# The first turn of an inverse transform in tiles of 32 rows by 64 columns, and some idle products in small tile shapes

## The chip, the cores and the metric

The kernel runs on one NeuronCore of one Trainium2 chip. It is one launch, with the inputs and the output in device memory, everything in float32. The metric is the device time of one execution in microseconds (us). Three executions of the kernel before took 675.04, 676.41 and 678.37 us; the median, 676.41 us, is its time.

The engines are called PE (TensorE, products into PSUM), DVE (VectorE), ACT (ScalarE), POOL (GpSimd) and SP (SyncE, here only a queue of transfers).

## The reference

Two residual blocks over 2048 tokens of 640 channels, with modulation rows computed from a vector `c`. Cut to what matters:

```python
x = A_q                                                     # (1, 2048, 640)
mod = (silu(c) @ w_mod).reshape(1, 6, 1, -1)                # sa, ca, ga, sb, cb, gb
h = layernorm(x) * (1 + ca) + sa
x = x + ga * A(h, A_k, A_v, A_shift_k, A_ssm_k, A_ssm_D)    # first block
h = layernorm(x) * (1 + cb) + sb
x = x + gb * B(h, B_w1, B_b1, B_w2, B_b2)                   # second block

def A(q, k, v, shift_k, ssm_k, ssm_D):
    kv = short_causal_conv(k, shift_k) * v                  # 4 taps in each channel
    y = irfft(rfft(kv, 4096) * rfft(ssm_k, 4096))[:2048]    # long causal convolution per channel
    return q * (y + kv * ssm_D)

def B(x, w1, b1, w2, b2):                                   # mixes tokens, channel by channel
    h = layernorm(x)
    u = gelu(einsum("bsd,sf->bdf", h, w1) + b1)             # 1728 hidden units
    return (einsum("bdf,fs->bds", u, w2) + b2).transpose(0, 2, 1)
```

## The kernel before

The first 280 us are block A, the rest block B. Block A works on channels in five chunks of 128, numbered 0 to 4 (`for c in range(NC)`, NC = 5). The long convolution of a chunk is a transform in two turns, a pointwise product and an inverse in two turns, all of them as f32 products on PE:

- `step1(side, t)` (line 223): the first turn forward, of the kernel (`side` 1) or of `kv` (`side` 0); 16 products a call with weights of 128 rows by 64 columns and 128 moving columns, four calls (`t`) for each side. ACT copies the result to `Z` (line 229).
- `f2(g)` (line 242): the second turn forward, 32 products a call with weights of 128 rows by 64 columns and 64 moving columns, in the two column halves of the array in turn; eight calls a chunk. ACT copies one half of each result (line 246), DVE multiplies both spectra (`mul`, line 57), POOL adds into `Y` (`add`).
- `i2(r)` (line 271): the first turn of the inverse, two calls a chunk, 64 products each. The 128 rows of `Y` are four independent strips of 32 rows (`qd`); a product takes 32 rows of `Y`, two of its columns blocks `i` at a time, as 128 weight columns, and 64 columns of the constant `V2` as the moving side. Each strip has its own PSUM bank. Four copies on ACT (line 280; in the last chunk's second call two of them on DVE, line 278) bring the result to `T2`.
- `i1(half)` (line 291): the second turn of the inverse, two calls a chunk, 64 products each with weights of 64 rows by 64 columns, in the four quarters of the array in turn. DVE multiplies the result by the modulated `q` straight from PSUM (`gate`).

All the order is written by hand; each engine works through its own list. In chunks 1 to 3 the list of PE is: eight `f2`, `step1(0,0)`, `step1(0,1)`, `i2(0)`, `step1(0,2)`, `i2(1)`, `step1(0,3)`, `i1(0)`, `step1(1,0)`, `i1(1)`, `step1(1,1)` to `step1(1,3)`, where `step1` already works for the next chunk. ACT's list there has the copies of `step1(0,0)` and `(0,1)`, the reordering of the next chunk's kernel (`perm`, line 168, two instructions), the four copies of `i2(0)`, the copy of `step1(0,2)`, the four of `i2(1)`. In chunk 0 the products for the modulation rows (`mod_part`, line 351) follow `step1(0,3)` on PE, and `mod_row` (362) after them gives the rows `G0`, `G1` that the gated product needs. In chunk 4 `mod_part` stands between the two calls of `i2`.

PSUM is eight banks: a ring of three slots of two banks, taken in turn by each call of `psum()`, and one slot for the taps. `i2` takes two slots, the others one.

At the very start PE has ten products of 128 x 128 by 512 columns whose result nobody reads (line 497, called idle products below), while the inputs are loaded; the first real work on PE is `step1(1,0)`.

The lines that the change touches, with the functions around them:

Of the kernel before, what the change touches and what calls it, by code (L numbers as in the profile page):

```python
# [47 lines left out]
def mixer_kernel(ctx: ExitStack, tc: tile.TileContext, q, k, v, shift_k, ssm_k, ssm_D, w1, b1, w2, b2, c,  # L48
# [7 lines left out]
    act, dve, pool, pe, sync = nc.scalar, nc.vector, nc.gpsimd, nc.tensor, nc.sync  # L56
# [3 lines left out]
    def mem(tag, n, name=None):  # L60

        return sb.tile([128, n], F32, name=name or tag, tag=tag, bufs=1)
# [4 lines left out]
    def psum(slot=None):  # L67

        uid[0] += 1
        slot = ring[uid[0] % len(ring)] if slot is None else slot  # L70
        return psp.tile([128, 1024], F32, name=f"pst_{uid[0]}", tag=f"pst{slot}", bufs=1)
# [5 lines left out]
    T_in, P, X, T_aux, T_kt = mem("in", 4288), mem("p", 2048), mem("x", 2048), mem("aux", 4096), mem("kt", 1536)  # L77
# [18 lines left out]
    Y = T_y.rearrange("p (r i k) -> p r i k", r=2, i=32)  # L96
# [3 lines left out]
    F1, V2, ID, OWN = SM[:, 0:256], SM[:, 256:384], SM[:, 384:420], SM[:, 420:422]  # L100
# [46 lines left out]
    def load_taps(c, eng=sync):  # L147
        for h in range(2):
            eng.dma_start(TR[64 * h:64 * h + 64], dram(shift_k, (DC * c + 64 * h) * 4, [[0, 64], [1, 256]]))
# [26 lines left out]
    def kv_ops(g, eng=dve, x=X, kx_=KX):  # L176
        S_, T_, W_ = (SV, TV, TAP) if eng is dve else (PS_.rearrange("p (n i) -> p n i", i=64),
                                                       PT.rearrange("p (n i) -> p n i", i=64), PW)
        pairs = lambda t: t.rearrange("p n (i e) -> p n i e", e=2)
        w = lambda s: W_[:, None, s, :].to_broadcast([128, 8, 64])  # L180
        kx = lambda s: kx_[:, 8 * g + 3 - s:8 * g + 11 - s, :]
        ops = [lambda: TT(eng, S_, kx(3), w(3), ALU.mult)]
        for s in (2, 1, 0):
            ops.append(lambda s=s: TT(eng, T_, kx(s), w(s), ALU.mult))
            ops.append(lambda: TT(eng, S_, S_, T_, ALU.add))
        ops.append(lambda: TT(eng, x.rearrange("p (i n e) -> p n i e", i=32, e=2)[:, 8 * g:8 * g + 8],
                              pairs(S_), pairs(VX[:, 8 * g:8 * g + 8]), ALU.mult))
        return ops
# [74 lines left out]
    def i2(r, eng=None):  # L263

        pp = [psum(), psum()]
        for s in range(8):
            for ri in range(2):
                for qd in range(4):
                    p = slice(32 * qd, 32 * qd + 32)
                    o, i = 512 * (qd % 2) + 64 * s, 2 * (8 * r + s)  # L270
                    pe.matmul(pp[qd // 2][:, o:o + 64], Y[p, ri, i:i + 2].rearrange("p i k -> p (i k)"),  # L271
                              V2[p, 64 * ri:64 * ri + 64], start=ri == 0, stop=ri == 1)
        for qd in range(4):
            a = 16 * (qd // 2) + 8 * r
            o = T2[:, a:a + 8, :, qd % 2]
            i = pp[qd // 2][:, 512 * (qd % 2):512 * (qd % 2) + 512].rearrange("p (a m) -> p a m", a=8)
            if eng is not None and qd > 1:
                eng.tensor_scalar(o, i, 1.0, None, op0=ALU.mult)
            else:
                act.activation(o, i, AF.Copy)  # L280

    def i1(half, slot=None):

        ps = psum(slot)
        for jj in range(8):
            for ri in range(2):
                for e in range(2):
                    p = slice(64 * e, 64 * e + 64)
                    for b in range(2):
                        n2 = 16 * b + 8 * half + jj  # L290
                        pe.matmul(ps[64 * b:64 * b + 64, 512 * e + 64 * jj:512 * e + 64 * jj + 64],  # L291
                                  V1[p, ri, n2], T2[p, :, 32 * ri + n2], start=ri == 0, stop=ri == 1)
        return ps
# [198 lines left out]
    w2_load(0)  # L492
    all_taps()
    load_taps(1, pool)
    ps = psum()
    for _ in range(10):
        pe.matmul(ps[:, 0:512], T_in[:, 192:320], T_in[:, 192:704], start=True, stop=True)
    ops = kv_ops(1, pool, X0)
    run(ops[:5])
    perm_add(0)  # L500
# [48 lines left out]
    for c in range(NC):  # L549
# [44 lines left out]
        if c == 0:  # L594
# [3 lines left out]
            ps = psum()  # L598
            pe.transpose(ps[:, 0:36], stg, ID[0:36, 0:36])
            act.activation(cols, ps[:, 0:36], AF.Copy)  # L600
            act.activation(sil, cols[:, 30:35], AF.Silu)
            step1(0, 1)
            i2(0)
            step1(0, 2)
            i2(1)
            k0 = step1(0, 3, True)
            for kk in range(4):
# [50 lines left out]
        if c:  # L658
            dv(7 if cn is not None else 8)
            i2(0)  # L660
            if cn is None:
                mod_part(tap, 3, pl[3])
                i2(1, dve)
                t = mem("y", 4096, "wb2")
                blk[2] = j16(t[:, 0:2048]), j16(t[:, 2048:4096])
                split_rows(0, X, (2,))
                split_rows(1, T_aux[:, 0:2048], (2,))
                break
            run(po)
            step1(0, 2)  # L670
            i2(1)
            step1(0, 3)
            dv(3)
# [11 lines left out]
        for half in range(2):  # L685
            ps = i1(half)
# [37 lines left out]
    start = []  # L724
# [84 lines left out]
    ps = i1(1, s1)  # L809
# [151 lines left out]
    for f_ in range(4, NF - 1):  # L961
        if f_ == HALF:
            ps = psum().rearrange("p (h m) -> p h m", h=2)
# [5 lines left out]
        ps = psum().rearrange("p (h m) -> p h m", h=2)  # L969
# [131 lines left out]
    for s in range(NW):  # L1101
        i = NF + s
# [16 lines left out]
        for f_ in range(NF):  # L1119
            u = U[f_]  # L1120
            for k, (w, r) in enumerate(((wh, 0), (wh, 2), (wl, 0))):
                for h in range(2):
                    pe.matmul(acc[s][:, h, 0:320], w[:, f_].bitcast(F32R), u[r + h].bitcast(F32R),  # L1123
                              start=f_ == 0 and k == 0, stop=f_ == NF - 1 and k == 2)
# [39 lines left out]
def build(inputs):  # L1164
    import concourse.bacc as bacc

    nc = bacc.Bacc("TRN2", target_bir_lowering=False, num_devices=1)
    arrays, args = {}, []

    def add(name, a):  # L1170
        a = np.ascontiguousarray(a)
        arrays[f"in_{name}_dram"] = a
        args.append(nc.dram_tensor(f"in_{name}_dram", a.shape, mybir.dt.from_np(a.dtype), kind="ExternalInput").ap())

    for name in _INS:
        a = np.asarray(inputs[name])
        add(name, a.reshape(S, D) if name in ('A_q', 'A_k', 'A_v') else a)
    for name, a in _constants().items():
        add("const_" + name, a)
    args.append(nc.dram_tensor("out_0_dram", (S, D), F32, kind="ExternalOutput").ap())  # L1180
    with tile.TileContext(nc) as tc:
        mixer_kernel(tc, *args)
    return nc, arrays
# [8 lines left out]
```

## Time and profile before

| what | value |
|---|---|
| executions | 675.04, 676.41, 678.37 us |
| profiled execution, from first to last instruction | 673.9 us (its span is the only time that it has) |
| PE matmuls | 628.9 us busy, 9119 records |
| PE weight loads | 596.1 us busy, 9119 records |
| DVE, ACT, POOL | 497.5, 300.1, 133.5 us busy |
| line 242 (`f2`), matmul | 2560 records, 78.9 us busy, median length of one 222 ns |
| line 271 (`i2`), matmul | 1280 records, 40.2 us busy, median length of one 270 ns |
| line 291 (`i1`), matmul | 1280 records, 23.6 us busy, median length of one 216 ns |
| line 223 (`step1`), matmul | 1280 records, 78.3 us busy |
| line 497 (idle products), matmul | 20 records, 11.4 us busy, first at 6.06 us |
| packets of the instruction queue q8 | 71, 1.16 MB |
| mean granted PE clock | 0.979 of full |

One product of f32 in the code is two matmul records and two weight loads in the trace (line 271: 10 calls of 64 products, 1280 records). Matmuls overlap, so the length of one record is not the time that it costs; the distance from one start to the next is. The times of block A's chunks, by the starts of `f2`: chunk 0 at 35.1 us, 1 at 98.9, 2 at 147.95, 3 at 191.55, 4 at 237.66; block B's products begin at 281 us.

In the rows below, an idle time is given in brackets with what ended it; "issue" there means that the profile shows nothing that the engine waited for. Names are output<-input.

### The profile page before, as it was taken

To read this page: it belongs to the slowest core of one execution; us is meant where nothing else is said; L and a number is where in the kernel's file an instruction comes from. 1 tells how busy PE (TensorE), PEld (TensorE's weight loads), DVE (VectorE), ACT (ScalarE), POOL (GpSimd) and SP (SyncE) were. 2 spreads that over 40 slices of the span, in tenths; PEclk is the share of its full clock that TensorE was granted. 3 is DMA by queue.
4 is the path that set the end of the run, shared out by engine and by line. 5 is a ranking of instruction groups with operands and counts; after the bars stand their busy time and mean duration, and the time that the engine had idled before them with its cause. 6 is when DMAs were issued, how large, how long until landed. Compare 5 with 4: busy or idle time off the path is not lost.

```text
span 673.9 us, 20760 instructions
## 1 busy us (share of the span) xinstructions
PE 628.9 (93%) x9119; PEld 596.1 (88%) x9119; DVE 497.5 (74%) x869; ACT 300.1 (45%) x483; POOL 133.5 (20%) x157
## 2 busy tenths in 40 slices
PE   6878887999999998999899999999999999999997
PEld 2878576989989996799789889999999999999997
DVE  7798698889798379788866621231589969888895
ACT  1564474647557465447654222322344143333331
POOL 5772068126133241000000000000000430000000
PEclk9999899999999999698999999999999999999999
DMA  9999897475426252430308333334352626356601
GB/s 185 214 266 259 277 181 160 94 147 115 67 66 217 60 154 65 107 81 1 63 3 154 63 62 65 63 63 116 98 147 71 190 77 182 115 147 168 187 32 39
DMA packets 166538, 81.23 MB, mean 121 GB/s; under 512 B 90830, under 2 KB 156912, under 8 KB 166448
## 3 DMA queue, kind: packets, MB, share of 16 engines
q1 hardware_dynamic: 159276, 78.32, 47.8%
q10 hardware_dynamic: 6916, 1.31, 1.2%
q8 instruction: 71, 1.16, 0.7%
q0 software_dynamic: 256, 0.28, 0.2%
q14 instruction: 19, 0.16, 0.1%
HBM read 69.40 MB, written 10.49 MB: 119 GB/s over the span
## 4 chain that ended last, share of the span: by engine, by line
PE 67%; DVE 16%; ACT 6%; issue 4%; DMA 3%; SPq 2%; POOL 1%; ACTq 0%; DVEq 0%; POOLq 0%
PE pst L445 20%; PE pst L1046 16%; PE pst L1123 7%; PE pst L223 7%; PE pst L271 6%; PE pst L242 6%; DVE p L57 2%; PE pst L291 2%; ACT z L280 2%; DVE tap L57 2%; PE tap L351 2%; PE pst L919 1%; DVE kt L57 1%; DMA y<-in_A_ssm_k_dram 1%; DVE aux L57 1%
## 5 line engine op out<-in xcount | busy, mean ns | idle before, releaser
L242 PE MATMUL pst<-z,w 128*64 128x64 f32 x2560 | 78.9, 223 | 13.5 <-DVE p L57 7.6
L242 PEld LDWEIGHTS pst<-z,w 128*64 128x64 f32 x2560 | 76.7, 138 | 16.3 <-issue 8.8
L57 POOL TENSOR_TENSOR y<-p 128x256 f32<-128x256 f32 x72 | 51.2, 740 | 39.7 <-DVE p L57 39.4
L229 ACT ACTIVATE z<-pst 128x1024 f32<-128x1024 f32 (+2 forms) x45 | 43.0, 974 | 35.0 <-PE pst L223 34.9
L57 DVE TENSOR_TENSOR p<-pst,kt 128x512 f32<-128x512 f32 x80 | 50.7, 680 | 8.6 <-ACT kt L246 8.6
L882 ACT ACTIVATE pst<-pst,sm 128x640 f32<-128x640 f32 x13 | 10.0, 766 | 75.8 <-PE pst L445 75.8
L271 PEld LDWEIGHTS pst<-v,y 32*128 32x128 f32 x1280 | 38.2, 187 | 6.0 <-issue 5.6
L271 PE MATMUL pst<-v,y 32*128 32x64 f32 x1280 | 40.2, 272 | 3.0 <-issue 2.9
L1046 PE MATMUL pst<-r_z,m_w 128*128 128x320 f32 x222 | 41.6, 309 | 0.1
L246 ACT ACTIVATE kt<-pst 128x512 f32<-128x512 f32 x40 | 23.9, 597 | 33.9 <-PE pst L242 17.1
L223 PE MATMUL pst<-v,p 128*64 128x128 f32 x640 | 36.7, 274 | 1.6 <-ACT p L168 1.6
L223 PEld LDWEIGHTS pst<-v,p 128*64 128x64 f32 x640 | 34.8, 137 | 3.0 <-ACT p L168 2.6
L57 POOL TENSOR_TENSOR m_p<-u_i,r_z 128x320 f32<-128x320 f32 x1 | 0.9, 870 | 183.4 <-issue 183.4
L1034 ACT ACTIVATE m_w<-m_v 128x896 fp32r<-128x896 f32 x24 | 22.7, 951 | 31.5 <-PE pst L1046 16.8
L57 DVE TENSOR_TENSOR tap<-tap,kt 128x512 f32<-128x512 f32 x51 | 35.5, 697 | 1.3
L223 PE MATMUL pst<-v,x 128*64 128x128 f32 x512 | 34.2, 291 | 2.0 <-issue 1.5
L1046 PEld LDWEIGHTS pst<-r_z,m_w 128*128 128x128 f32 x222 | 34.8, 188 | 0.4 <-DVE m_w L57 0.4
L223 PEld LDWEIGHTS pst<-v,x 128*64 128x64 f32 x512 | 30.9, 147 | 3.2 <-issue 2.5
L280 ACT ACTIVATE z<-pst 128x512 f32<-128x512 f32 x38 | 20.9, 644 | 24.0 <-PE pst L271 24.0
L57 DVE TENSOR_TENSOR m_w<-m_v,m_w 128x896 fp32r<-128x896 f32 x24 | 27.9, 1165 | 2.5 <-ACT m_w L1034 2.1
L57 DVE TENSOR_TENSOR kt<-in,tap 128x512 f32<-128x512 f32 x42 | 28.8, 686 | 1.2
L445 PE MATMUL pst<-r_z,wb0b 128*128 128x320 f32 x180 | 28.2, 310 | 0.9 <-DVE u_x L57 0.9
(308 smaller groups left out, 1497.5 us busy)
## 6 DMA issues: line engine op xcount, KB each, us to landing
x<-in_B_w_dram SPq DMA_DIRECT2D x20, 512.0 KB
m_x<-xs SPq DMA_DIRECT2D x28, 160.0 KB
out_dram<-m_x SPq DMA_DIRECT2D x28, 160.0 KB
aux<-in_A_ssm_k_dram SPq DMA_DIRECT2D x8, 512.0 KB
m_v<-in_B_w_dram SPq DMA_DIRECT2D x9, 448.0 KB
in<-in_w_mod_dram SPq DMA_DIRECT2D x4, 960.0 KB
x<-in_B_w_dram SPq DMA_DIRECT2D x7, 448.0 KB
in<-in_A_v_dram SPq DMA_DIRECT2D x22, 128.0 KB
```

The lines of the kernel that those rows point to most:

```text
L57: TT = lambda eng, o, a, b, op: eng.tensor_tensor(o, a, b, op=op)
L223: pe.matmul(ps[64 * ri:64 * ri + 64, o:o + 255:2], lhs, F1[:, 128 * ri:128 * ri + 128], start=True, stop=True)
L229: act.activation(Z[:, side, t, :, k0:k1], ps.rearrange("p (a k e) -> p a k e", a=4, e=2)[:, :, k0:k1], AF.Copy)
L242: pe.matmul(ps[64 * h:64 * h + 64, o:o + 64], W2[k1 // 32][:, 2 * (k1 % 32) + ri], rhs, start=True, stop=True)
L246: act.activation(kt.rearrange("p (m i) -> p m i", i=32), pv[:, :, 1], AF.Copy)
L271: pe.matmul(pp[qd // 2][:, o:o + 64], Y[p, ri, i:i + 2].rearrange("p i k -> p (i k)"), V2[p, 64 * ri:64 * ri + 64], start=ri == 0, stop=ri ...
L280: act.activation(o, i, AF.Copy)
L291: pe.matmul(ps[64 * b:64 * b + 64, 512 * e + 64 * jj:512 * e + 64 * jj + 64], V1[p, ri, n2], T2[p, :, 32 * ri + n2], start=ri == 0, stop=r ...
L445: pe.matmul(ps[0:m, h, 0:320], w_.bitcast(F32R), r_[:, 320 * h:320 * h + 320].bitcast(F32R), start=first and i == 0, stop=last and i == 2)
L1034: act.activation(W[n][0].bitcast(F32R), A[p, w_], AF.Copy)
L1046: pe.matmul(bank[n], w[:, i].bitcast(F32R), r.bitcast(F32R), start=i == 0 and k == 0, stop=i == 6 and k == 2)
L1123: pe.matmul(acc[s][:, h, 0:320], w[:, f_].bitcast(F32R), u[r + h].bitcast(F32R), start=f_ == 0 and k == 0, stop=f_ == NF - 1 and k == 2)
```

## The change

`i2` gets a loop over `e`. Instead of two column blocks of `Y` as 128 weight columns, a product takes one as 64 weight columns, and writes PSUM partitions 0 to 63 (`e` = 0) or 64 to 127 (`e` = 1), that is through the left or the right column half of the array. The four row strips and the moving side stay as they are, and so do the PSUM banks, the copies behind and all their waits. A call has 128 products where it had 64.

Of the ten idle products five stay. The others are replaced by 64 products with 64 moving columns: 16 in tiles of 64 x 64, 32 in tiles of 64 rows by 32 columns, 16 in tiles of 64 x 64 that write every second PSUM column. For these a second PSUM slot is taken, which turns the ring of three on by one for everything behind.

```diff
@@ i2 @@
         for s in range(8):
             for ri in range(2):
-                for qd in range(4):
-                    p = slice(32 * qd, 32 * qd + 32)
-                    o, i = 512 * (qd % 2) + 64 * s, 2 * (8 * r + s)
-                    pe.matmul(pp[qd // 2][:, o:o + 64], Y[p, ri, i:i + 2].rearrange("p i k -> p (i k)"),
-                              V2[p, 64 * ri:64 * ri + 64], start=ri == 0, stop=ri == 1)
+                for e in range(2):
+                    for qd in range(4):
+                        p = slice(32 * qd, 32 * qd + 32)
+                        o, i = 512 * (qd % 2) + 64 * s, 2 * (8 * r + s) + e
+                        pe.matmul(pp[qd // 2][64 * e:64 * e + 64, o:o + 64], Y[p, ri, i],
+                                  V2[p, 64 * ri:64 * ri + 64], start=ri == 0, stop=ri == 1)
@@ before the first kv_ops @@
-    ps = psum()
-    for _ in range(10):
-        pe.matmul(ps[:, 0:512], T_in[:, 192:320], T_in[:, 192:704], start=True, stop=True)
+    ps, ps_ = psum(), psum()
+    kin = T_in[:, 192:704]
+    for _ in range(5):
+        pe.matmul(ps[:, 0:512], kin[:, 0:128], kin, start=True, stop=True)
+
+    lo = lambda a: slice(64 * a, 64 * a + 64)
+    for n in range(16):
+        a, b, o = n // 2 % 2, n % 2, 64 * (n // 4)
+        pe.matmul(ps[lo(b), 512 * a + o:512 * a + o + 64], kin[lo(a), o:o + 64], kin[lo(a), 256:320], start=True, stop=True)
+    for n in range(32):
+        a, b, o = n // 4 % 2, n % 4, 64 * (n // 8)
+        pe.matmul(ps[32 * b:32 * b + 32, 512 * a + o:512 * a + o + 64], kin[lo(a), o:o + 32], kin[lo(a), 256:320], start=True, stop=True)
+    for n in range(16):
+        a, b, o = n // 2 % 2, n % 2, 128 * (n // 4)
+        pe.matmul(ps_[lo(b), 512 * a + o:512 * a + o + 128:2], kin[lo(a), o // 2:o // 2 + 64], kin[lo(a), 256:320], start=True, stop=True)
```

Line 271 of the kernel before is line 272 after it, and the lines behind the idle products move on by 13.

On PE the list of chunk 2, from `step1(0,1)` to `i1(0)`, reads before (the shape is that of the output, `x2` means two calls in a row; of each call of `i2` the first two rows are shown, for strips 0 and 1 in one slot and 2 and 3 in the other, and 30 like them follow):

```order
L223 MATMUL pst_2486<-v,x 64x128 x16
L271 MATMUL pst_2513<-v,y 128x64 x2
L271 MATMUL pst_2514<-v,y 128x64 x2
...
L223 MATMUL pst_2585<-v,x 64x128 x16
L271 MATMUL pst_2603<-v,y 128x64 x2
L271 MATMUL pst_2604<-v,y 128x64 x2
...
L223 MATMUL pst_2673<-v,x 64x128 x16
L291 MATMUL pst_2698<-z,v 64x64 x64
```

and after the change (here 62 rows like the two shown follow in each call):

```order
L223 MATMUL pst_2802<-v,x 64x128 x16
L272 MATMUL pst_2829<-v,y 64x64 x2
L272 MATMUL pst_2830<-v,y 64x64 x2
...
L223 MATMUL pst_2965<-v,x 64x128 x16
L272 MATMUL pst_2983<-v,y 64x64 x2
L272 MATMUL pst_2984<-v,y 64x64 x2
...
L223 MATMUL pst_3117<-v,x 64x128 x16
L292 MATMUL pst_3142<-z,v 64x64 x64
```

The order of the calls is the same; a call of `i2` has 128 products for 64, each with an output of 64 partitions for 128.

At the start of PE's list, before:

```order
L497 MATMUL pst_125<-in 128x512 x10
L223 MATMUL pst_189<-v,p 64x128 x16
L223 MATMUL pst_207<-v,p 64x128 x16
L223 MATMUL pst_225<-v,p 64x128 x16
L223 MATMUL pst_243<-v,p 64x128 x16
```

and after:

```order
L499 MATMUL pst_125<-in 128x512 x5
L504 MATMUL pst_125<-in 64x64 x16
L507 MATMUL pst_125<-in 32x64 x32
L510 MATMUL pst_126<-in 64x64 x16
L223 MATMUL pst_249<-v,p 64x128 x16
```

Five products of 512 columns have gone, 64 of 64 columns have come; what follows is the same.

## The prediction, made before the changed kernel was run

> **What bounds the kernel now.** I read the stages first, then the timeline of TensorE (PE), then what ends its idle time. The view of busy time by stage (stage: length, PE, PE weight loads, DVE, ACT, POOL, granted clock, DMA share, GB/s):
>
> ```profile
> 148.00:164.00 16.00, 15.32 (x512) 15.11 (x514) 15.76 (x26) 10.17 (x22) 8.73 (x14) 1.00 0.58 138
> 164.00:179.60 15.60, 15.39 (x392) 14.54 (x387) 12.34 (x16) 11.40 (x18) 1.86 (x3) 1.00 0.59 105
> ```
>
> 148 to 164 us is `f2` of channel chunk 2, with DVE and PE both full; 164 to 179.6 us holds that chunk's two calls of `i2`, and there PE alone is full. The timeline of PE through that stage (start, length, what, idle time before):
>
> ```profile
> 164.02 3.69 PE L223 MATMUL pst<-v,x 128*64 128x128 f32 x64
> 167.64 3.80 PE L271 MATMUL pst<-v,y 32*128 32x64 f32 x128
> 171.37 1.97 PE L223 MATMUL pst<-v,x 128*64 128x128 f32 x32
> 173.27 4.29 PE L271 MATMUL pst<-v,y 32*128 32x64 f32 x128
> 177.49 1.97 PE L223 MATMUL pst<-v,x 128*64 128x128 f32 x32
> 179.65 1.56 PE L291 MATMUL pst<-z,v 64*64 64x64 f32 x90 [0.19 <-ACT z L280]
> ```
>
> So line 271 stands on the path here. What a product costs is read from whole stretches: the first row of line 271 above, and of lines 291 and 242
>
> ```profile
> 179.65 2.10 PE L291 MATMUL pst<-z,v 64*64 64x64 f32 x128 [0.19 <-ACT z L280]
> ...
> 147.95 2.14 PE L242 MATMUL pst<-z,w 128*64 128x64 f32 x66 [0.49 <-ACT z L229]
> ```
>
> One f32 product in the code is two records (64 calls in `i2`, 128 records), each a weight load and a matmul; I call such a record a pair. Less the length of one (0.27, 0.22 and 0.22 us, in the table ahead) the paces are 27.8, 14.8 and 29.5 ns a pair. Times the number of tiles in turn (4 row strips; 4 quarters; 2 column halves) each tile is held 111, 59 and 59 ns: twice as long where the weights have 128 columns as where they have 64.
>
> There is a second limit, and PE shows it as idle time that no engine ends. The chain of waits in chunk 0, and then the timeline of PE in that chunk's `i2` stage and in its two calls of `i1`:
>
> ```profile
> 43.10 3.89 PE pst L242 x126
> 46.99 1.44 issue
> 48.44 3.95 PE pst L242 x127
> 52.38 0.62 issue
> 53.01 1.91 PE pst L242 x57
> ```
>
> ```profile
> 64.70 1.91 PE L223 MATMUL pst<-v,x 128*64 128x128 f32 x30 [1.50 <-issue]
> 66.54 3.00 PE L271 MATMUL pst<-v,y 32*128 32x64 f32 x97
> 71.30 1.12 PE L271 MATMUL pst<-v,y 32*128 32x64 f32 x31 [1.77 <-issue]
> ...
> 84.46 3.84 PE L291 MATMUL pst<-z,v 64*64 64x64 f32 x246
> 89.39 0.44 PE L291 MATMUL pst<-z,v 64*64 64x64 f32 x10 [1.09 <-issue]
> ```
>
> The stops lie 127 pairs apart (126 and 127 above; 30 and 97 make 127). The page's counts say what that is:
>
> ```profile
> PE 628.9 (93%) x9119; PEld 596.1 (88%) x9119; DVE 497.5 (74%) x869; ACT 300.1 (45%) x483; POOL 133.5 (20%) x157
> ...
> q8 instruction: 71, 1.16, 0.7%
> ```
>
> 71 packets of 16 KB carry 9119 pairs: 128 pairs a packet. PE stops where a packet of its instructions is missing. How fast packets come is read from the DMA view in narrow windows, here 87 to 88 us, 168.9 to 170.1 us and 224.4 to 231.4 us (packets, MB, share of 16 engines):
>
> ```profile
> q8 instruction: 1, 0.02, 5.8%
> ...
> q8 instruction: 1, 0.02, 4.8%
> ...
> q8 instruction: 3, 0.05, 2.9%
> ```
>
> The packet that ends the stop at 88 us is moved between 87 and 88 us, in 0.93 us (5.8% of 16 engines in 1 us), and PE goes on at 89.39, some 1.4 us after. No other is moved before 90.8 us, though PE stands empty: the next one is asked for only when the one before is in use. One at a time, a packet costs 0.93 + 1.4 us and some 1.3 us until the next moves, about 3.6 us. In the window at 224 us the starts lie 3.4 us apart on average; while chunk 0's loads run, PE's restarts are 5.3 (43.10 to 48.44), 4.6 (48.44 to 53.01) and 6.6 us (64.70 to 71.30) apart. At 3.6 us a packet PE gets a pair each 28 ns. Lines 271 and 242 want one each 28 to 29.5 ns, just what comes; line 291 wants twice as much and lives on stock, 128 pairs at a time. That stock is seen at 84.46: the packet moved at 87 us was asked for 1.3 to 1.6 us before, when some 70 of the 246 pairs were done. So PE has about 176 pairs left, 1.4 packets, when it asks.
>
> **The change part by part.** Line 271 makes 128 products a call where it made 64: 256 pairs for 128, ten times, 1280 pairs or ten packets more. Each has 64 weight columns. *What a pair takes.* No row has 32 rows by 64 columns on eight tiles. From below: every tile is held 59 ns as in lines 291 and 242, eight in turn, 7.4 ns; a call then takes 1.9 us for 3.55. From above: the two column halves of a strip don't overlap, 14.8 ns, 3.8 us a call. Line 242 has both halves on the same rows and runs them at once (29.5 is half of 59), so I take 7.4. Left to itself that would be up to 1.65 us off each call.
>
> *What it is fed.* Chunk 2, from the start of `i2(0)` (167.64) to the end of `i1(0)` (179.65 + 2.10): now 128 + 32 + 128 + 32 + 128 = 448 pairs in 14.1 us. The change needs 704, 5.5 packets. At its start PE has asked (the packet in 168.9 to 170.1 us), so 1.4 packets are in stock and the next is usable after some 3.7 us. It needs 4.1 more, so five: the fifth is there at 3.7 + 4 x 3.6 = 18.1 us, the last pairs take 0.3, 18.4 us for 14.1: 4.3 us more. With 3.3 us a packet it is 3.1 more, with the loaded 4.6 it is 8.3. ACT's copies fall into the stops and add nothing. Chunks 1 and 3 have the same order: 3 x 4.3 = 13 us. The bounds are 9 and 25; I put 20 at the top, since these stages carry less load than chunk 0.
>
> Chunk 0 starves already, so its two packets more cost their whole time, 4.6 to 6.6 us each while the loads run. The stage's end now falls later, when the loads thin out, and I take 4.5 each, 9 us (6 to 13). What stands behind it is on the path: the modulation products (L351) follow `i2` on PE, and the gate rows, the gated product and so the next chunk wait for them. Chunk 4:
>
> ```profile
> 257.10 3.93 PE L271 MATMUL pst<-v,y 32*128 32x64 f32 x128
> 260.96 1.28 PE L351 MATMUL tap<-z,sm 128*32 128x320 f32 x12
> 262.16 1.45 PE L271 MATMUL pst<-v,y 32*128 32x64 f32 x41
> 264.08 2.68 PE L271 MATMUL pst<-v,y 32*128 32x64 f32 x87 [0.47 <-issue]
> ```
>
> These 268 pairs in 9.7 us become 524, 4.1 packets. Less 1.4 in stock it needs three: 0.3 + 3 x 3.6 + 0.4 = 11.5 us, 2 us more (0 to 5).
>
> *The clock.* In chunk 3, after a stop in `i2`, the chain of waits has 32 pairs of line 223 in 3.39 us where the row at 171.37 has 1.97, and that stage's granted clock is 0.96:
>
> ```profile
> 216.34 3.39 PE pst L223 x32
> ```
>
> ```profile
> 191.50:237.70 46.20, 43.98 (x1282) 42.31 (x1282) 31.96 (x67) 25.91 (x44) 15.39 (x18) 0.96 0.40 113
> ```
>
> Longer stops give more such stretches, but most of their 1.4 us passes while a packet is awaited anyway. I put 2 us in all (0 to 6).
>
> *The idle products* end earlier: five of 512 columns go, 64 small ones (128 pairs) come.
>
> ```profile
> 6.06 11.37 PE L497 MATMUL pst<-in 128*128 128x512 f32 x20 [6.06 <-DMA in<-in_A_k_dram]
> 17.69 1.53 PE L223 MATMUL pst<-v,p 128*64 128x128 f32 x24 [0.27 <-ACT p L168]
> ```
>
> At 17.69 us PE waits for ACT anyhow. I take nothing; if the clock falls in the longer idle time it is one slow stretch, 1.4 us at most. Their 118 pairs net are fetched in that idle time.
>
> The sum: 13 + 9 + 2 + 2 = 26 us on the profiled 673.9 us; the runs' median lies 2.5 us above that span, so 676.4 + 26 = 702 us. The lower bounds (9 + 6) give 691, the upper (20 + 13 + 5 + 6) 720.
>
> A page of the Trainium skill would have it otherwise: "Runtime: NRT & Kernel Launch", section Instruction fetch mechanics, says that instructions are refilled in 16 KiB blocks and that crossing a border is mostly hidden. By it the sum would be that of the first rival below; the stops of 1.09 to 1.77 us above contradict it.
>
> **The rivals.** *The stream keeps up* (0.11): packets come faster once PE asks faster, and eight tiles run at 7.4 ns. For it: no row shows a demand like this for as long. Against it: no packet moved while PE stood empty at 88 us. Its price in a middle chunk: the first call ends 1.65 us earlier, but ACT is busy until 170.85 with the rows below, so its copies start only 0.6 us earlier; the second call gives its whole 1.65.
>
> ```profile
> 168.71 2.14 ACT L168 ACTIVATE p<-aux 128x1024 f32<-128x1024 f32 x2
> 171.48 2.25 ACT L280 ACTIVATE z<-pst 128x512 f32<-128x512 f32 x4 [0.63 <-PE pst L271]
> ```
>
> That is 3 x 2.25, 3.3 in chunk 0 and 2 in chunk 4: 12 us less, 664 us. It decides once a packet takes less than about 2.7 us: five of them then end with the 14.1 us of now.
>
> *Half overlap, and fed* (0.05): 14.8 ns a pair gives 0.26 us more a call, 3 us in all, 679 us, no change that can be told. For it: eight tiles at once are in no row; against it the stops.
>
> *One tile after another* (0.06): the halves of a strip block each other, and a pair takes some 28 ns. For it: that is what a pair of line 271 takes now. Against it: lines 242 and 291, whose halves overlap. A call takes 7.1 us, 3.6 more, ten times: 712 us. The Trainium skill's page "TensorE: Matmul & The Clock Gate", section Back-to-back issue gap, has an issue floor of about 25 ns for such small products; by it 2560 x 25 = 64 us stand for the 36 of now, an estimate of 704 us. Line 291's 14.8 ns speaks against that floor.
>
> **How the numbers follow.** The forecast, slower through the instruction stream, has 0.78, the rivals 0.11, 0.05 and 0.06. About 0.5% (3.4 us) is what a measurement of this kernel can tell from no change. Slower is 0.78 + 0.06 = 0.84, the same 0.05, faster 0.11. The likeliest one's own range is 691 to 720; I go down to 686, since other engines may take up part of the delay, and end at 718. The rival at 712 lies inside, those at 664 and 679 outside.
>
> **What would show it.** Right: idle stretches "issue" of 1 to 3 us between bursts of 128 pairs of line 272; packets of q8 up from 71 to 81 or 82 and about 3.6 us apart through the `i2` stages; inside a burst a pace near 7.4 ns; chunk 2's stretch 18 us for 14, chunk 0's stage some 9 longer. Wrong: `i2` calls of under 2.5 us without such idle time (first rival), or calls of 3.8 or 7 us without it (the others).

## The result, and the profile after

The changed kernel takes 711.12 us (median; 708.93 to 713.52) where the kernel before takes 677.39 (675.04 to 683.15) beside it: 1.0486 times as long, 95% interval 1.0433 to 1.0538, or 34 us more. Its profiled execution has a span of 711.7 us, against 673.9, at a mean granted clock of 0.953, against 0.979.

The counts, the instruction queue, the chain's shares and the costliest groups on the page of after:

```profile
PE 632.8 (89%) x10517; PEld 599.5 (84%) x10517; DVE 498.9 (70%) x869; ACT 300.8 (42%) x483; POOL 133.8 (19%) x157
...
q8 instruction: 82, 1.34, 0.8%
...
PE 64%; DVE 17%; issue 8%; DMA 5%; ACT 4%; SPq 1%; POOL 1%; ACTq 0%; DVEq 0%; POOLq 0%
...
L272 PE MATMUL pst<-v,y 32*64 32x64 f32 x2560 | 37.6, 256 | 27.3 <-issue 27.0
```

The chain and line 271 on the page of before:

```profile
PE 67%; DVE 16%; ACT 6%; issue 4%; DMA 3%; SPq 2%; POOL 1%; ACTq 0%; DVEq 0%; POOLq 0%
...
L271 PE MATMUL pst<-v,y 32*128 32x64 f32 x1280 | 40.2, 272 | 3.0 <-issue 2.9
```

PE has hardly more to do (632.8 us of busy time for 628.9), and line 272 takes less of it than line 271 did (37.6 for 40.2 us). What is new is idle time that no engine ends: 27.0 us of "issue" ahead of line 272, where there are 2.9 ahead of line 271 before. The instruction queue moved 82 packets for 71: 1398 more pairs are 10.9 packets of 128. In the chain that ended last, "issue" has 8% of the span, where before it has 4%.

Busy time by chunk, from one chunk's start of `f2` to the next (columns as in the prediction's first fence), before, for chunk 2:

```profile
147.95:191.55 43.60, 42.17 (x1281) 40.55 (x1281) 38.95 (x55) 26.26 (x45) 15.38 (x18) 1.00 0.50 105
```

and after, for chunks 0 to 4, with the rest of the kernel in the last row:

```profile
35.20:115.10 79.90, 59.15 (x1609) 51.82 (x1609) 57.47 (x106) 37.67 (x59) 29.25 (x36) 0.81 0.78 206
115.10:168.30 53.20, 43.37 (x1536) 40.86 (x1537) 39.35 (x55) 26.57 (x45) 20.03 (x20) 0.97 0.54 110
168.30:219.04 50.74, 43.15 (x1536) 40.86 (x1536) 39.01 (x55) 26.34 (x45) 15.36 (x18) 0.97 0.43 91
219.04:271.30 52.26, 43.72 (x1536) 41.12 (x1536) 31.92 (x67) 25.79 (x44) 15.37 (x18) 0.93 0.35 100
271.30:318.30 47.00, 39.02 (x1352) 32.10 (x1352) 35.24 (x84) 22.73 (x49) 10.22 (x15) 0.89 0.30 85
...
318.30:711.70 393.40, 378.53 (x2555) 371.42 (x2554) 270.67 (x463) 148.21 (x231) 19.45 (x26) 0.99 0.39 97
```

In chunk 2 PE is busy 43.15 us where it was 42.17, but the chunk is 7.1 us longer: PE had 1.4 us of idle time in it and now has 7.6. Chunks 0 to 4 are 16.1, 4.1, 7.1, 6.2 and 3.2 us longer than before (where they take 63.8, 49.05, 43.6, 46.1 and 43.8 us), and all that follows is 0.9 us longer. Chunks with the old products lie up to 2.5 us apart in the profiled executions of the experiments below, and chunk 0 over 5 (63.8 to 69.2 us), so a chunk alone is a rough measure. The `i2` stages, which hold the change, are sharper in chunks 1, 2 and 4; in chunk 3 they take 16.5 to 19.1 us with the old products, in chunk 0 13.1 to 19.5.

The timeline of PE in chunk 2's `i2` stage after (before: the second fence of the prediction):

```profile
188.02 2.15 PE L272 MATMUL pst<-v,y 32*64 32x64 f32 x179
191.91 1.09 PE L272 MATMUL pst<-v,y 32*64 32x64 f32 x77 [1.74 <-issue]
192.93 1.97 PE L223 MATMUL pst<-v,x 128*64 128x128 f32 x32
194.83 0.82 PE L272 MATMUL pst<-v,y 32*64 32x64 f32 x18
196.13 1.58 PE L272 MATMUL pst<-v,y 32*64 32x64 f32 x128 [0.48 <-issue]
200.69 1.87 PE L272 MATMUL pst<-v,y 32*64 32x64 f32 x110 [2.97 <-issue]
202.48 3.00 PE L223 MATMUL pst<-v,x 128*64 128x128 f32 x32
205.41 1.96 PE L292 MATMUL pst<-z,v 64*64 64x64 f32 x114
208.24 0.46 PE L292 MATMUL pst<-z,v 64*64 64x64 f32 x14 [0.86 <-issue]
```

PE runs through its stock of 179 pairs in 2.15 us and stops. From then on it gets 128 pairs at a time: 77 + 32 + 18 make 127, then 128, then 110 and 18 of the 32, then 14 + 114. These are four packets in 208.24 - 191.91 = 16.33 us, 4.1 us each. Inside a burst a pair takes (1.58 - 0.26) / 127 = 10.4 ns. The 32 pairs at 202.48 take 3.00 us for 1.97: a stretch of lower clock after the stop of 2.97 us (0.64 granted from 200.7 to 205.5 us).

And chunk 0's stage after:

```profile
61.78 1.76 PE L272 MATMUL pst<-v,y 32*64 32x64 f32 x140
67.10 1.73 PE L272 MATMUL pst<-v,y 32*64 32x64 f32 x116 [3.55 <-issue]
68.75 1.55 PE L223 MATMUL pst<-v,x 128*64 128x128 f32 x12
73.30 2.40 PE L223 MATMUL pst<-v,x 128*64 128x128 f32 x20 [2.99 <-issue]
75.63 1.99 PE L272 MATMUL pst<-v,y 32*64 32x64 f32 x107
79.87 2.25 PE L272 MATMUL pst<-v,y 32*64 32x64 f32 x128 [2.25 <-issue]
83.32 0.69 PE L272 MATMUL pst<-v,y 32*64 32x64 f32 x21 [1.21 <-issue]
83.94 3.68 PE L223 MATMUL pst<-v,x 128*64 128x128 f32 x32
```

Here the packets come 6.2 (67.10 to 73.30) and 6.6 us apart (73.30 to 79.87) while the loads run, and then 3.5 (79.87 to 83.32). The 32 pairs at the end take 3.68 us for 1.97: PE is at half its clock (0.50 granted from 74 to 88 us).

The same stages in both kernels, from the first pair of `i2(0)` to the end of `i1(0)` in chunks 1 to 3, to the end of the second `i2` in chunk 4, and to the last `step1` in chunk 0, all read from such timelines of PE:

| chunk | before, us | after, us | more | forecast |
|---|---|---|---|---|
| 0 | 59.03 to 75.84: 16.8 | 61.78 to 87.62: 25.8 | 9.0 | 9 |
| 1 | 123.69 to 137.80: 14.1 | 137.76 to 157.95: 20.2 | 6.1 | 4.3 |
| 2 | 167.64 to 181.75: 14.1 | 188.02 to 208.70: 20.7 | 6.6 | 4.3 |
| 3 | 211.37 to 227.86: 16.5 | 238.76 to 260.98: 22.2 | 5.7 | 4.3 |
| 4 | 257.10 to 266.76: 9.7 | 290.76 to 305.06: 14.3 | 4.6 | 2 |
| sum | | | 32.0 | 24 and 2 for the clock |

These 32 us, in stages that are a seventh of the span, are most of the 37.8 by which the two profiled executions differ (the medians differ by 34). What is left lies mostly in chunk 0, ahead of its stage (2.7 us) and behind it (4.4), where executions with the old products differ from each other as much.

### The profile page after: what moved, and what is told of

It reads as the page before. It is cut to its first block, busy times and chain, and to the rows that moved or that the text cites. A ratio compares the mean times of both kernels' runs of the same rounds, so it can differ in the third digit from the quotient of the medians.

```text
span 711.7 us, 23556 instructions
## 1 busy us (share of the span) xinstructions
PE 632.8 (89%) x10517; PEld 599.5 (84%) x10517; DVE 498.9 (70%) x869; ACT 300.8 (42%) x483; POOL 133.8 (19%) x157
## 4 chain that ended last, share of the span: by engine, by line
PE 64%; DVE 17%; issue 8%; DMA 5%; ACT 4%; SPq 1%; POOL 1%; ACTq 0%; DVEq 0%; POOLq 0%
PE pst L446 19%; PE pst L1059 15%; PE pst L223 8%; PE pst L1136 7%; PE pst L272 5%; PE pst L242 5%; DVE p L57 3%; PE pst L292 2%; DVE tap L57 2%; DVE aux L57 1%; PE tap L352 1%; DVE kt L57 1%; PE pst L932 1%; DMA y<-in_A_ssm_k_dram 1%; DVE sm L561 1%
## 5 line engine op out<-in xcount | busy, mean ns | idle before, releaser
L242 PE MATMUL pst<-z,w 128*64 128x64 f32 x2560 | 81.0, 226 | 10.4 <-DVE p L57 6.0
L242 PEld LDWEIGHTS pst<-z,w 128*64 128x64 f32 x2560 | 79.0, 142 | 12.9 <-issue 9.2
L272 PE MATMUL pst<-v,y 32*64 32x64 f32 x2560 | 37.6, 256 | 27.3 <-issue 27.0
L272 PEld LDWEIGHTS pst<-v,y 32*64 32x64 f32 x2560 | 33.7, 150 | 32.7 <-issue 31.2
L57 DVE TENSOR_TENSOR p<-pst,kt 128x512 f32<-128x512 f32 x80 | 50.8, 683 | 10.9 <-ACT kt L246 10.8
L223 PE MATMUL pst<-v,p 128*64 128x128 f32 x640 | 41.0, 293 | 7.2 <-DVE aux L57 4.0
L223 PEld LDWEIGHTS pst<-v,p 128*64 128x64 f32 x640 | 39.1, 149 | 7.8 <-issue 4.1
L223 PE MATMUL pst<-v,x 128*64 128x128 f32 x512 | 38.1, 310 | 5.3 <-issue 3.9
L281 ACT ACTIVATE z<-pst 128x512 f32<-128x512 f32 x38 | 20.7, 639 | 47.0 <-PE pst L272 47.0
L223 PEld LDWEIGHTS pst<-v,x 128*64 128x64 f32 x512 | 33.9, 158 | 7.0 <-issue 5.1
L1047 ACT ACTIVATE m_w<-m_v 128x896 fp32r<-128x896 f32 x24 | 22.7, 951 | 31.4 <-PE pst L1059 16.8
L292 PE MATMUL pst<-z,v 64*64 64x64 f32 x1280 | 25.5, 234 | 6.7 <-issue 5.2
L292 PEld LDWEIGHTS pst<-z,v 64*64 64x64 f32 x1280 | 23.3, 148 | 9.6 <-issue 7.5
L57 DVE TENSOR_TENSOR aux<-pst,aux 128x1024 f32<-128x1024 f32 (+2 forms) x11 | 12.4, 1123 | 26.1 <-PE pst L292 25.8
```

The source lines that it names most:

```text
L57: TT = lambda eng, o, a, b, op: eng.tensor_tensor(o, a, b, op=op)
L223: pe.matmul(ps[64 * ri:64 * ri + 64, o:o + 255:2], lhs, F1[:, 128 * ri:128 * ri + 128], start=True, stop=True)
L242: pe.matmul(ps[64 * h:64 * h + 64, o:o + 64], W2[k1 // 32][:, 2 * (k1 % 32) + ri], rhs, start=True, stop=True)
L272: pe.matmul(pp[qd // 2][64 * e:64 * e + 64, o:o + 64], Y[p, ri, i], V2[p, 64 * ri:64 * ri + 64], start=ri == 0, stop=ri == 1)
L1047: act.activation(W[n][0].bitcast(F32R), A[p, w_], AF.Copy)
```

## The experiments

The theory is the prediction's: the loss is the fetching of ten packets more, each worth some 3.6 us of PE's time, and not the work of the products. Against it stand that the products' own pace or shape is the cost, and that the idle products are.

**One half of the change at a time.** First the new `i2` alone, with the old idle products (the edit against the changed kernel):

```diff
-    ps, ps_ = psum(), psum()
-    kin = T_in[:, 192:704]
...
+    ps = psum()
+    for _ in range(10):
+        pe.matmul(ps[:, 0:512], T_in[:, 192:320], T_in[:, 192:704], start=True, stop=True)
```

> The kernel before with the new products of i2 alone (the ten idle products as before). Theory 1, the instruction stream: everything comes from the 1280 pairs more, so 711 us like the whole change, within 4. Theory 3, the start of the program (idle time, clock, the PSUM ring turned by one): a part of the loss is missing, below 705.

Measured: 712.61 us against 677.47, ratio 1.0517 (1.0482 to 1.0553), 35 us. The new products of `i2` hold the whole loss.

Then the kernel before with the new idle products alone (the second piece of the diff, without the first):

> The kernel before with the new idle products alone. Theory 1: no change, 677 us within 3 (118 pairs more are fetched while PE waits anyway). Theory 3: over 682.

Measured: 680.67 us against 677.47, ratio 1.0047 (1.0012 to 1.0081). That is 3.2 us (0.8 to 5.5), at the edge of what can be told, just over the expected 677 within 3 and more than the 1.4 us that the prediction allowed. The first products of line 223 in this kernel:

```profile
18.46 9.48 PE L223 MATMUL pst<-v,p 128*64 128x128 f32 x128 [4.39 <-ACT p L168]
```

PE now waits 4.39 us for ACT and then runs its first 128 pairs in 9.48 us, where the kernel before takes 7.21 (17.69 to 24.90). The granted clock from 18.5 to 28 us is 0.76: behind the longer wait PE is slower. But the start of `f2` in chunk 0 moves by a few tenths only (35.43 us for 35.13), and in the first experiment the old idle products saved nothing. Where the other 3 us would be is open.

**The count alone.** If packets are the cost, it must come without the new shape as well, and go when the shape stays and the count is halved. First 64 tiny products (8 moving columns, results unused) ahead of each call in the kernel before, in the new tile shape: also 1280 pairs.

```diff
+        for n in range(64):
+            qd, e = n % 4, n // 4 % 2
+            p = slice(32 * qd, 32 * qd + 32)
+            pe.matmul(pp[qd // 2][64 * e:64 * e + 64, 512 * (qd % 2):512 * (qd % 2) + 8], F1[p, 0:64], F1[p, 0:8],
+                      start=True, stop=True)
         for s in range(8):
             for ri in range(2):
                 for qd in range(4):
```

> The kernel before, its i2 untouched, with 64 small products (8 moving columns, 32 rows by 64 columns) ahead of each call: as many records as the change adds, their results overwritten. Their own work is 128 pairs of some 11 ns and two changes of tile shape, 1.8 us a call, 18 us in all if they are fed. Theory 1: 128 pairs more a call cost what the change costs, 705 to 720 us. Theory 2, the work and the tile shape cost the time and not the count: at most 695.

Measured: 734.92 us against 677.47, ratio 1.0844 (1.0757 to 1.0931), 57 us: above both theories' numbers. The rival, that pairs with little work cost only their own time, is out: the tiny products (line 269) are busy 15.8 us in all. But the loss has another form than in the change. The old products (line 276 here) on the page:

```profile
L276 PE MATMUL pst<-v,y 32*128 32x64 f32 x1280 | 63.7, 370 | 10.8 <-issue 10.8
```

Their idle time "issue" grows by 8 us only, from 2.9 to 10.8, while they are busy 63.7 us for 40.2, and all of PE 680.5 for 628.9. So most of the 57 us is PE at work, and slow. The timeline of PE in chunk 0 and the clock's row of the page:

```profile
57.99 1.52 PE L269 MATMUL pst<-v 32*64 32x8 f32 x128
59.44 0.43 PE L276 MATMUL pst<-v,y 32*128 32x64 f32 x3
62.79 6.81 PE L276 MATMUL pst<-v,y 32*128 32x64 f32 x125 [2.92 <-issue]
69.53 3.68 PE L223 MATMUL pst<-v,x 128*64 128x128 f32 x32
```

```profile
PEclk9997789879879859957999999999999999999999
```

After a stop of 2.92 us the old products take some 53 ns a pair where they took 28, and `step1` 3.68 us for 1.97: the work behind the stop ran at half the clock (mean granted clock 0.922). The ten packets would be 36 us at 3.6 each, but a pair of 53 ns is slower than packets come, so here much of the waiting is hidden under the slow work and the two costs can't be told apart. The run shows that the count costs time, not that each packet costs 3.6 us.

Now the change with half the products: the new tiles of 32 rows by 64 columns as they are, but each product over all 128 columns of V2's rows, for half of the `s` (its sums aren't those of the reference):

```diff
-        for s in range(8):
+        for s in range(4):
...
-                        o, i = 512 * (qd % 2) + 64 * s, 2 * (8 * r + s) + e
-                        pe.matmul(pp[qd // 2][64 * e:64 * e + 64, o:o + 64], Y[p, ri, i],
-                                  V2[p, 64 * ri:64 * ri + 64], start=ri == 0, stop=ri == 1)
+                        o, i = 512 * (qd % 2) + 128 * s, 2 * (8 * r + s) + e
+                        pe.matmul(pp[qd // 2][64 * e:64 * e + 64, o:o + 128], Y[p, ri, i],
+                                  V2[p], start=ri == 0, stop=ri == 1)
```

> The changed kernel with half as many products in each i2 call, each with 128 moving columns for 64 in the same tiles of 32 rows by 64 columns (the sums are not those of the reference: both constants are applied to every block of half the blocks). The columns moved stay the same, the count is that of the kernel before. Theory 1: 665 to 680 us. Theory 2: the tiles stay slow, 695 or more.

Measured: 676.83 us against 677.47, ratio 1.0003 (0.9977 to 1.0028). The group of line 272 in the answer by lines, and the instruction queue:

```profile
L272 PE MATMUL pst<-v,y 32*64 32x128 f32 x1280 | 24.9, 287 | 7.4 <-issue 5.6 <-ACT z L281 1.8
```

```profile
q8 instruction: 72, 1.18, 0.7%
```

Same tiles and as many moving columns in all, in half the pairs: the loss is gone, and so are 10 of the 82 packets. PE is even busy 15 us less with this line than with line 271 (24.9 for 40.2), and the kernel still gains nothing.

**More work, same stream.** If PE waits for packets anyway, long products in the middle of a call are free. The change, with four products of 128 by 128 over 192 columns in each call (results unused):

```diff
         for s in range(8):
+            for _ in range(4 if s == 4 else 0):
+                pe.matmul(pp[0][:, 320:512], F1[:, 0:128], F1[:, 0:192], start=True, stop=True)
             for ri in range(2):
                 for e in range(2):
```

> The changed kernel with four long products (128 x 128 by 192 columns) in the middle of each call, their results overwritten: 8 pairs of 160 ns and two changes of shape, 1.7 us of work a call, 17 us in all. Theory 1: they run while PE would stand for want of instructions and keep the clock up, so 711 us within 6. Theory 2, work bounds the stage: 725 or more.

Measured: 711.69 us against 678.31, ratio 1.0504 (1.0444 to 1.0564), what the change has without them. Its timeline of PE in chunk 2:

```profile
181.19 1.59 PE L274 MATMUL pst<-v,y 32*64 32x64 f32 x128
182.72 1.57 PE L268 MATMUL pst<-v 128*128 128x192 f32 x8
184.21 2.03 PE L274 MATMUL pst<-v,y 32*64 32x64 f32 x128
```

Ten calls with 1.5 us of work more, some 15 us in all, cost nothing that this measurement can tell (its interval is some 4 us either way): the products stand where the stop stood. The mean clock is 0.973, higher than the 0.953 of the change. So, in chunk 2 at least, the lower clock isn't what costs the time either: its stage takes 19.8 us here (181.19 to 201.03) with the full clock granted from 180 to 200 us, and 20.7 in the change.

**The price of a packet.** 1024 pairs in the new tile shape after the last product of the kernel before, with nothing else to do (results unused):

```diff
+    for m in range(2):
+        ps = [psum(), psum()]
+        for n in range(256):
+            qd, e = (n % 4, n // 4 % 2) if m == 0 else (n // 2 % 4, n % 2)
+            p = slice(32 * qd, 32 * qd + 32)
+            pe.matmul(ps[qd // 2][64 * e:64 * e + 64, 512 * (qd % 2):512 * (qd % 2) + 64], us[0][0][p, 0:64], us[0][0][p, 64:128],
+                      start=True, stop=True)
```

> The kernel before with 512 products of 32 rows by 64 columns, 64 moving columns, behind its last product, 256 in the order of the change (the strips of one column half, then of the other) and 256 with both column halves of a strip in turn. 1024 pairs are eight packets, while hardly any data moves. Theory 1: one packet at a time, 3.4 to 3.7 us each, 27 to 30 us longer than before. If packets came as fast as PE asks: 1024 pairs of some 11 ns, 11 us longer. Inside a burst the first order should show the 10.8 ns of the change; a shorter pace in the second would be the order's doing.

Measured: 704.26 us against 678.31, ratio 1.0386 (1.0315 to 1.0456), 26 us more, just under the 27 to 30 expected. The timeline of PE at its end:

```profile
672.75 1.83 PE L1165 MATMUL pst<-u_t 32*64 32x64 f32 x148
675.70 1.59 PE L1165 MATMUL pst<-u_t 32*64 32x64 f32 x128 [1.12 <-issue]
679.17 2.26 PE L1165 MATMUL pst<-u_t 32*64 32x64 f32 x128 [1.88 <-issue]
...
697.35 2.01 PE L1165 MATMUL pst<-u_t 32*64 32x64 f32 x108 [1.21 <-issue]
```

The stream in its pure form: 128 pairs, a stop, 128 pairs. Seven restarts from 675.70 to 697.35 are (697.35 - 675.70) / 6 = 3.6 us apart. Inside a burst a pair takes 10.8 ns at full clock ((1.59 - 0.22) / 127), and some 16 from 679 us on, where the granted clock is 0.50; the distance of packets stays 3.5 to 3.8 us. The order of the products, which differs between the two halves of the tail, makes no difference (bursts of 2.26 us at 679.17 and at 690.13).

The same tail with 16 loads of 1 MB issued beside it (their data is not used):

```diff
+    for n in range(16):
+        load_rows(n % 3, (X, m_v[:, 0:2048], m_v[:, 2048:4096])[n % 3])
```

> The kernel before with the same 1024 pairs behind its last product as in the run with the quiet tail, while 16 loads of 1 MB each (2 KB rows, into buffers that nothing reads any more) run. The time itself may be set by the loads; what counts is the distance of the packets of q8. If the load of the DMA queues is what makes a packet cost 4.1 us in chunk 2 and 4.6 to 7 us in chunk 0 where the quiet tail has 3.6 us: 4.5 us or more a packet here. If not (something in those stages, waits of PE's list or the slower clock): 3.6 us here too.

Measured: 761.43 us, where the kernel before took 675.88. Its timeline of PE, and busy time by window (DMA share in the last column but one):

```profile
696.74 2.33 PE L1167 MATMUL pst<-u_t 32*64 32x64 f32 x128 [6.68 <-issue]
705.69 2.26 PE L1167 MATMUL pst<-u_t 32*64 32x64 f32 x128 [6.62 <-issue]
```

```profile
690.00:720.00 30.00, 6.91 (x388) 6.30 (x384) 0.00 (x0) 0.00 (x0) 0.00 (x0) 0.50 1.07 221
```

With the DMA engines full, restarts are 705.69 - 696.74 = 8.95 us apart instead of 3.6, and the next ones as far. The granted clock is 0.50 in both tails from the second restart on, so the clock isn't the difference: the price of a packet is a matter of what else the DMA engines carry.

**Where in the kernel.** The change in chunks 1 to 4 alone, with the old products in chunk 0:

```diff
-                for e in range(2):
+                for e in range(2 if i2c[0] > 2 else 1):
...
+                        if i2c[0] < 3:
+                            pe.matmul(pp[qd // 2][:, o:o + 64], Y[p, ri, i:i + 2].rearrange("p i k -> p (i k)"),
+                                      V2[p, 64 * ri:64 * ri + 64], start=ri == 0, stop=ri == 1)
+                            continue
```

> The changed kernel with the old products in chunk 0 and the new ones in chunks 1 to 4. Theory 1: the 16 us that chunk 0 is longer come back, 695 us within 4, and the other chunks keep their 3 to 7 us. Were the loss one of the whole program (clock, code size), more than half of it would stay evenly, above 702.

Measured: 703.54 us against 678.31, ratio 1.0371 (1.0319 to 1.0422): 25 us of the 34 stay, where some 17 were expected, and the time lies just above the 702 from which the expectation would have had a loss of the whole program. The trace shows no such spread: the stages of chunks 1 to 4 take 19.9, 20.0, 23.6 and 15.1 us, 24 more than before in all, and what follows chunk 4 takes 393.5 us for 392.5. The expectation of 17 rested on the 16 us by which chunk 0 was longer in the one profiled execution. Chunk 0 here takes 69.2 us, and the two ratios put its part at 34 - 25 = 9 us, with several us either way, as its stage does in the table above.

The new products only in the first of the two calls of each chunk (`for e in range(2 if r == 0 else 1)`, and the old product where `r` is 1), five packets more instead of ten:

> The changed kernel with the new products in the first call of i2 of each chunk and the old ones in the second: five packets more than before in place of ten. If each packet more costs its own time, because the stages of block A have no slack left in the instruction stream: half the loss, 691 to 698 us. If a stage can make up for one packet more from its stock and only the second one costs: under 688 us.

Measured: 699.7 us against 675.88, ratio 1.035 (1.0299 to 1.0401): 24 us, more than half of the loss, and just over the expected range. Chunk 0's stage takes 25.6 us (59.62 to 85.23), as much as with the whole change: its clock is down at 0.50, and the old products of the second call take 7.11 us there for 3.80. In chunks 1 to 4 the stage is 2.6, 2.8, 1.9 and 4.0 us longer than before, where both calls make it 6.1, 6.6, 5.7 and 4.6 longer; with chunk 0's 8.8 that is 20.1 us, and this execution's span is 20.5 longer. So the packets aren't worth the same: one more in chunk 0's loaded stage or in chunk 4 costs nearly all, one more in chunks 1 to 3 less than its 3.6 us. That the old call behind it covers the rest is a reading of these stages, not an experiment.

**Fewer packets.** If packets bound chunk 0 before the change, products of two strips with half the count should gain there. The kernel before, with `i2` of chunks 0 to 3 as products of 64 rows by 128 columns against a copy of V2 in blocks (zeros elsewhere):

```diff
+                    for hf in range(2):
+                        p = slice(64 * hf, 64 * hf + 64)
+                        i = 2 * (8 * r + s)
+                        pe.matmul(pp[hf][:, 128 * s:128 * s + 128], Y[p, ri, i:i + 2].rearrange("p i k -> p (i k)"),
+                                  V2B[p, 128 * ri:128 * ri + 128], start=ri == 0, stop=ri == 1)
```

> The kernel before with i2 of chunks 0 to 3 as products of 64 rows by 128 columns: two strips in one product, the moving side a constant with the two strips' blocks on its diagonal, 128 columns. Half as many records (512 pairs, four packets less), each tile held twice as long, the same result. PE's own time stays as it was (tiles of 111 ns, two of them in turn, 64 pairs: 3.55 us a call). Theory 1: the stops of chunk 0 and chunk 3 shrink, 3 to 8 us less than before, 670 to 674 us. Theory 2: no difference, 677.

Measured: 678.76 us against 678.31, ratio 1.0011 (0.9981 to 1.0041): no gain, where 3 to 8 us were expected. The end of chunk 0's stage in its timeline of PE:

```profile
69.17 1.97 PE L224 MATMUL pst<-v,x 128*64 128x128 f32 x32
71.07 1.28 PE L367 MATMUL tap<-v,sm 128*32 128x320 f32 x12
...
74.75 1.28 PE L367 MATMUL tap<-aux,sm 128*32 128x320 f32 x12 [1.12 <-DMA aux<-in_w_mod_dram]
...
80.31 1.28 PE L367 MATMUL tap<-p,sm 128*32 128x320 f32 x12 [1.73 <-DMA p<-in_w_mod_dram]
```

The stops are gone and the modulation products start at 71.07 us, where the kernel before has them at 75.77. But now they wait for the loads of their weights, and the product of line 378 that follows them (362 in the kernel before) begins at 82.40 us, where it began at 82.26. So in the kernel before, the stops of the stream in this stage seem to hide a DMA wait about as long, read from one execution, and a gain would have to mend both.

## Why the prediction held, and where its sum was short

Direction and cause held: slower through the instruction stream (0.78, and 0.84 for slower), 711 us inside 686 to 718. The likeliest sum said 26 us; it is 34. The terms that were too small are the packet's price in chunks 1 to 3 (18.4 us for 13) and the first restart of chunk 4 (4.6 for 2). Step by step:

- **A packet is 128 pairs, fetched one at a time, 3.6 us each.** Right, and the main reason: 82 packets for the 81 or 82 foretold, bursts of 128, restarts 3.6 us apart in the bare tail, and half the pairs in the same tiles cost nothing. 3.6 us is the price beside quiet DMA engines.
- **The middle chunks, 3 x 4.3 us.** Too small: 6.1, 6.6 and 5.7 us. The credit for stock was right: chunk 2's stage has 3.89 us until the first restart (188.02 to 191.91; 3.7 in the sum), then four packets, then 0.46 us of work. The term that was mis-sized is the packet: four take 16.33 us, 4.1 each, where the sum has 3.6. With 3.6 the stage would be 3.9 + 14.4 + 0.5 = 18.8 us, close to the 18.4 forecast. In chunks 1 and 3 the same reading gives 3.9 and 4.5 us a packet. The DMA row of after from 189 to 211 us (one digit for 0.55 us; the packets of instructions are at most a single 1 in it) shows what else moves there:

```profile
DMA  0100001899991069999400000000001000000010
```

  Two loads of 512 KB for `aux` fill about 192.6 to 195.6 and 196.7 to 200 us, and the longest stop ends at 200.69. The tail with loads shows that busy DMA engines make packets slow, so this is the likely reason; it wasn't tried in this place. The prediction had both prices for these stages (8.3 us more with a loaded packet) and took the quiet one.
- **Chunk 0, 9 us at 4.5 a packet.** The stage is 9.0 us longer, and the change without chunk 0 is some 9 us faster than the whole change. That it is 9.0 so exactly is luck: the stage takes 13.1 to 19.5 us in five executions with the old products, 25.8 and 26.9 in two with the new ones. The parts differ from the foretold: 6.2 and 6.6 us for two packets under load, then 3.5, and PE at half clock. The modulation products behind it start 75.77 to 87.55, 11.8 us later, of which 2.7 stood already at the stage's start.
- **Chunk 4, 2 us.** It is 4.6. The timeline of after:

```profile
290.76 2.47 PE L272 MATMUL pst<-v,y 32*64 32x64 f32 x191
296.72 1.29 PE L272 MATMUL pst<-v,y 32*64 32x64 f32 x65 [3.48 <-issue]
297.93 2.33 PE L352 MATMUL tap<-z,sm 128*32 128x320 f32 x12
300.19 2.15 PE L272 MATMUL pst<-v,y 32*64 32x64 f32 x179
303.97 1.09 PE L272 MATMUL pst<-v,y 32*64 32x64 f32 x77 [1.62 <-issue]
```

  From 296.72 to 303.97 are 65 + 12 + 179 pairs, two packets in 7.25 us, 3.6 each as assumed. The step that failed is the time to the first restart: 5.96 us, where the sum had 3.9. The prediction's own rows had it: before, the restart at 264.08 comes 6.98 us after the stage's start at 257.10, with 181 pairs between. The DMA row from 289 to 305 us (0.4 us a digit) has a load of 960 KB for line 352 in just that time:

```profile
DMA  0000000693989997200000100000000100000000
```

- **A pair at 7.4 ns inside a burst.** 10.4 to 10.8 ns at full clock, between the bounds of 7.4 and 14.8. It has hardly an effect: PE waits either way, as the free long products show. The rival of tiles one after another (28 ns) is out by this row. The Trainium skill's page "TensorE: Matmul & The Clock Gate", section Back-to-back issue gap, with its floor of about 25 ns would have given an estimate of 704 us, close to the time for another reason. The trace disagrees with the floor: 10.8 ns.
- **The clock, 2 us.** The half-speed stretches are there (202.48 and 83.94 above), and the stages' differences hold them; what they cost apart from the stops was not measured, in chunk 0 above all, where the clock is at 0.50. In chunk 2 the run with long products, at full clock, leaves them under 1 us (19.8 for 20.7). In the kernel with tiny products they cost much more.
- **The idle products, nothing, at most 1.4 us.** Alone 3.2 us (0.8 to 5.5); within the change no part of them is seen.
- **The stream keeps up (0.11) and half overlap, fed (0.05).** Both needed calls without stops. The Trainium skill's page "Runtime: NRT & Kernel Launch", section Instruction fetch mechanics, has crossing a 16 KiB block mostly hidden. The traces here agree only where PE wants pairs no faster than packets come: chunk 2 of the kernel before crosses ten borders without a stop for instructions, while the bare tail stops for 1.12 to 1.88 us at each.

## What to carry to other kernels

Count instructions as well as their time: here PE gets 128 weight-and-product pairs (16 KB) each 3.6 us when the DMA engines are quiet, 28 ns a pair, and 4 to 9 us when they are loaded. By these runs, splitting products into smaller tiles for concurrency can only gain while each pair keeps PE busy for longer than that; look for "issue" ahead of PE and for bursts of 128, and then make products fewer and longer. And where such stops are removed, look what waits beside them before counting a gain, as the load of weights did here.

## What the runs showed of the hardware that was not expected

- A full DMA side makes an instruction packet cost 8.95 us for 3.6. The transfer is no longer: one packet moves in 1.3 us in either tail (from 693.9 us loaded, from 680.3 quiet; 6.0% of 16 engines' time in 1.4 us, and 5.8%). The wait ahead of it grows: it begins 6.1 us after PE's last restart (687.78) in the loaded tail, 1.1 after it (679.17) in the quiet one.
- Stops from missing instructions go with a lower clock, as the wait for ACT does at the start (0.76 after 4.39 us): the bare tail runs at 0.50 from 679 us on, with stops of only 1.1 to 1.9 us.
- In these runs pairs on eight tiles come no closer than about 10 ns: 10.4 to 10.8 ns with 64 moving columns, (1.52 - 0.2) / 127 = 10.4 with 8 (the row at 57.99 us of the tiny products). That this is a limit on the issue of pairs is an argument from these two rows, not an experiment.
- Some 15 us of PE work put into the stops cost nothing that could be told, and the mean clock was 0.973 with them for 0.953.
